# Batches 0 and 1 of a Fourier mixing layer and its MLP forward in plain float32, with a reordered start and a new tie rule in the planner

## Chip, cores and metric

The kernel runs on one core of one Trainium2 chip. The metric is the device time of one launch in microseconds (us), as the median of several runs. The core has a matrix engine (PE, whose weight loads are listed apart as PEld), a vector engine (DVE), a scalar engine (ACT), GpSimd (POOL), and the queue of SyncE (SP), which issues all transfers here.

## What is computed

The reference has two parts. The input x has 8 batches of 3136 positions and 256 features.

```python
X = np.fft.rfft(x, axis=1)
Yr = Xr @ w_r - Xi @ w_i + b_r
Yi = Xr @ w_i + Xi @ w_r + b_i
lam = 0.01
Yr = np.sign(Yr) * np.maximum(np.abs(Yr) - lam, 0.0)
Yi = np.sign(Yi) * np.maximum(np.abs(Yi) - lam, 0.0)
y = np.fft.irfft(Y, n=x.shape[1], axis=1)
...
h = x @ w_in
sm = e / (np.sum(e, axis=-1, keepdims=True) + 1e-09)
solu = h * sm
ln = (solu - mu) / np.sqrt(var + 1e-06) * g_ln
return (ln @ w_out).astype(np.float32)
```

In the second part x is the 25088 rows of the first part's result, w_in is 256 x 1024 in float64, w_out is 1024 x 256 in float64, and e = exp(h - max h).

## The kernel before

**Transform.** 3136 = 98 x 32, so each batch is transformed in two steps by matrices. Step 1 (`fwd1`, for batch 0 `fwd1_first`) multiplies 98 rows by a 98 x 98 matrix, in 8 chunks c of 1024 columns, and writes the result `s1` to DRAM. Step 2 works in 13 units u of up to 128 rows: `load_bin` brings a group of 4 row blocks (2 units) back as the tile `bin`; `fwd2` multiplies it by the matrices `fb` into the tiles Xh, Xl; `mix` multiplies these by the mixing weights (tile yt, then y, split into yh and yl); `inv1` multiplies by `gb` and writes `s2` to DRAM. `inv2` reads `s2` (tile zt), multiplies by the 98 x 98 matrix `ia` and writes a ring of rows (`ring_hi`, `ring_lo`) for the MLP.

**Precision.** Operands are split in a high and a low half in float16, and each product is three matrix multiplications: high by high, high by low, low by high. The split costs one ACT copy and one DVE operation (Xh/Xl, xh/xl, zout, av). The scale of a split comes from the largest value of the batch: `load_peak` reads the batch once for that (8 loads, 8 DVE reductions `peaks`) before `fwd1` reads it again. In batch 0, step 1 is already one float32 multiplication (`fa_s`); `split_bin` then splits what step 2 reads (the tile `av`).

**MLP.** 196 tiles k of 128 rows. `moe_head` computes h in two halves of 512 columns (PSUM tile `ph`, 6 multiplications each), its maximum (`nm`), and exp and product (tile u). `moe_turn` splits u (lh by ACT, ll by POOL) and turns both by transposing transfers (th, tl). `moe_tail` multiplies by w_out (PSUM tile `po`, 24 multiplications). w_in and w_out arrive as float64 words; `load_wide` turns 512 columns of them into float32 in seven DVE operations (five of one input, tiles lh, ll, junk, and two of two inputs) and one on POOL. There are eight such conversions: four for w_in (`moe_w_in`), four for w_out (`moe_w_out`); `finish_w_in` and `finish_w_out` then scale and split them.

**Order.** All operations are recorded by `Plan`, which decides their order by a simulation with fixed costs per operation. Each operation carries a key (`nc.key`); on each engine, among the operations that can start within a tolerance of the earliest one, the lowest key is taken. The engine whose operation starts first is served; at a tie the first in `ENGINES` wins. Some DVE operations and all of POOL's take turns at one modelled port (`op.port`), so DVE and POOL often tie. `nc.hold` makes a transfer wait for another operation (`raw[b, g]`, the load of group g of batch b). All instructions are issued by one helper, so every row has the same line (L339 before, L342 after) and groups are told apart by their tiles.

Of the kernel before, what the change touches and what calls it, by code (L numbers as in the profile page):

```python
# [39 lines left out]
def fft_constants():  # L40
# [49 lines left out]
    out = dict(fa=FA.astype(np.float32))  # L90
# [145 lines left out]
class Plan:  # L236
# [3 lines left out]
    ENGINES = ("tensor", "vector", "scalar", "gpsimd", "sync")  # L240
# [100 lines left out]
    def order(self):  # L341
# [107 lines left out]
def fft_mix_solu_kernel(ctx: ExitStack, tc, x, w_r, w_i, b_r, b_i, w_in, w_out, g_ln, fa, fa16, fb, fs, gb, gs, ia, out):  # L449
# [81 lines left out]
    def load_peak(b, c):  # L531

        n = S * D // P // NPK
        t = xp.tile([P, C1], F32, name="xt", bufs=3)[:, :n]
        if b == 1 and c < 3:

            nc.hold(raw[0, 4])
        nc.sync.dma_start(t, x[b].rearrange("s d -> (s d)").rearrange("(p c n) -> c p n", p=P, c=NPK)[c])
        note_peak(b, c, NPK, t)

    def set_scales(b):
# [18 lines left out]
        nc.vector.tensor_scalar(sc[:, 4:], sc[:, :1], S_SCALE, None, ALU.mult)  # L560
# [7 lines left out]
            x=sc[:, 0:1], s=sc[:, 4:], lam=(sc[:, 2:3], sc[:, 3:4]), mix=un[:, 2:3], bias=bias_y, y=un[:, 1:2]  # L568
# [35 lines left out]
    def fwd1_first(c):  # L604


        if c == 0:
            s1[0] = dram.tile([N1, N2, D], F32, name="s1f")
        n2 = C1 // D
        xt = mp.tile([P, C1], F32, name="u", bufs=4)[:N1]  # L610
        nc.sync.dma_start(xt, x[0].rearrange("(n1 n2) d -> n1 (n2 d)", n1=N1)[:, c * C1 : (c + 1) * C1])
        note_peak(0, c, N2 // n2, xt)
        av = fp.tile([P, C1], F32, name=("zout", "bin")[c % 2], bufs=2)[:N1]
        for h in range(C1 // HF):
            hs = slice(h * HF, (h + 1) * HF)
            pa = front_psum(0)
            nc.reserve(av[:, hs])
            nc.tensor.matmul(pa[:N1], fa_s, xt[:, hs], start=True, stop=True)
            nc.scalar.copy(av[:, hs], pa[:N1])
        nc.sync.dma_start(s1[0][:, c * n2 : (c + 1) * n2], av.rearrange("p (n d) -> p n d", d=D))  # L620
# [8 lines left out]
    def load_bin(b, g):  # L629

        if b:
# [4 lines left out]
        v = s1[0][: 4 * Q].rearrange("(q c) n d -> q (c n) d", c=4).rearrange("q r d -> r q d")  # L636
# [19 lines left out]
    def fwd2(b, u):  # L656
        n, K = unit_size(u)
        if b not in s2:
            s2[b] = dram.tile([N1, N2 * 2 * D], F16, name="s2")
        if n == 1:  # L660
            bt, gi, fw = fp.tile([K, 1, 2, D], F16, name="bin_s", bufs=1), 0, [fs_s]
            if b:
                nc.sync.dma_start(bt[:, 0], s1[b][4 * Q :].rearrange("c n t d -> (c n) t d"))
            else:
                t = fp.tile([K, 1, D], F32, name="bin_f", bufs=1)
                nc.sync.dma_start(t[:, 0], s1[b][4 * Q :].rearrange("c n d -> (c n) d"))
                split_bin(bt, t)
        else:
# [11 lines left out]
        with nc.together():  # L680
            for i in range(n):
                for dh in range(ND):
                    ds = slice(dh * P, (dh + 1) * P)
                    for k, (t, j) in enumerate(((0, 0), (0, 1), (1, 0))):
                        nc.tensor.matmul(pv[:, :, dh, i], bt[:, gi + i, t, ds], fw[i][:, j], start=k == 0, stop=k == 2)

        if b:
            nc.scalar.activation(xs[:, :, :n], pv[:, 1, :, :n], AF.Copy, scale=B_SCALE)
        for r in range(2) if n == 1 else [slice(0, 2)]:
            nc.scalar.activation(xh[:, r, :, :n], pv[:, r, :, :n], AF.Copy, scale=B_SCALE)  # L690
            nc.vector.scalar_tensor_tensor(xl[:, r, :, :n], pv[:, r, :, :n], B_SCALE, xh[:, r, :, :n], ALU.mult, ALU.subtract)
        if b:
            nc.vector.scalar_tensor_tensor(xs[:, :, :n], pv[:, 0, :, :n], B_SCALE, xs[:, :, :n], ALU.mult, ALU.add)
# [50 lines left out]
    def mix(b, u):  # L744
# [6 lines left out]
        y = fp.tile([P, 2, D], F32, name="y", bufs=1)  # L751
# [13 lines left out]
    def inv1(b, u0, u1):  # L765
# [173 lines left out]
    for c in range(NCH):  # L939
        fwd1_first(c)  # L940
# [64 lines left out]
    nc.sync.dma_start(fb_s[0], fb[:, :QG])  # L1005
# [169 lines left out]
```

## Time and profile before

| | |
|---|---|
| median of 3 runs | 1658.26 us (1657.31 to 1661.03) |
| profiled execution, its own time | 1657.71 us |
| its span in the trace | 1655.8 us |
| busy: PE, DVE, ACT, POOL | 1581.2, 1381.2, 1244.9, 1134.9 us |
| mean granted PE clock | 0.982 of full speed |

The span is the time from the first to the last instruction in the trace; 1.9 us of the execution lie around it. A busy share of an engine counts the time in which at least one of its instructions runs.

### The profile page before, as it was taken

The page shows a single profiled execution, that of the slowest core. Times are in us where ns is not written, and L with a number is a line of the kernel's source. Part 1 is how long each engine was busy: PE and PEld are TensorE (multiplying, and loading weights), DVE is VectorE, ACT ScalarE, POOL GpSimd, SP SyncE. Part 2 cuts the span into 40 slices and gives each one's busy share as a digit, 9 for nine tenths or more (in the row PEclk, how much of TensorE's full clock was granted, in tenths as well). Part 3 has the DMA queues.
Part 4 walks back from the last instruction along what each step waited for, and adds up shares of the span by engine and source line. Part 5 has one row for each costly group of instructions (what it writes and reads, how often), then busy time and mean ns, then how long its engine had stood idle before and what let it go on. Part 6 is the DMA issues. An engine that isn't in the chain of part 4 may idle for free.

```text
span 1655.8 us, 38277 instructions
## 1 busy us (share of the span) xinstructions
PE 1581.2 (95%) x13220; PEld 1116.7 (67%) x13220; DVE 1381.2 (83%) x3399; ACT 1244.9 (75%) x2511; POOL 1134.9 (69%) x1889
## 2 busy tenths in 40 slices
PE   5777999999999999999999999999999999999998
PEld 3344677668775677667776577766777677766765
DVE  4999888997899968998779987899689878877775
ACT  3567876886777767887678886888678876777886
POOL 1464586768776678766776577776777767777666
PEclk8897999999999999999999999999999999999999
DMA  6735995799659987799857997689956986658766
GB/s 219 263 125 162 209 219 140 186 253 187 141 122 208 245 161 138 161 236 203 179 122 158 247 209 162 112 208 251 184 134 156 188 185 144 126 115 160 149 130 116
DMA packets 531267, 290.24 MB, mean 175 GB/s; under 512 B 425758, under 2 KB 502016, under 8 KB 531072
## 3 DMA queue, kind: packets, MB, share of 16 engines
q1 hardware_dynamic: 531072, 287.80, 79.0%
q8 instruction: 103, 1.69, 0.5%
q14 instruction: 92, 0.75, 0.1%
HBM read 107.88 MB, written 77.07 MB: 112 GB/s over the span
## 4 chain that ended last, share of the span: by engine, by line
PE 73%; DVE 8%; DMA 8%; ACT 4%; POOL 3%; issue 3%; SPq 0%; DVEq 0%; ACTq 0%; POOLq 0%
PE po L339 25%; PE ph L339 24%; PE pf L339 22%; DMA tl<-ll 2%; DMA th<-lh 2%; PE pb L339 2%; DVE u L339 1%; POOL ll L339 1%; DMA xt<-in_x_dram 1%; DVE yt L339 1%; DMA u<-in_x_dram 1%; DVE nm L339 1%; DMA zt<-s 1%; ACT u L339 1%; ACT junk L339 1%
## 5 line engine op out<-in xcount | busy, mean ns | idle before, releaser
L339 POOL TENSOR_TENSOR ll<-u,lh 128x1024 f16<-128x1024 f32 x196 | 425.4, 2170 | 113.5 <-ACT lh L339 107.8
L339 PE MATMUL po<-wout,th 128*128 128x256 f16 x3136 | 374.1, 273 | 6.6 <-DMA th<-lh 4.5
L339 PEld LDWEIGHTS <-th 128*128 128x128 f16 x3136 | 303.8, 98 | 69.4 <-DMA th<-lh 7.6
L339 ACT ACTIVATE u<-ph,m,hsb 128x512 f32<-128x512 f32 x384 | 295.9, 777 | 61.4 <-DVE m L339 58.7
L339 DVE TENSOR_REDUCE nm<-ph 128x1 f32<-128x512 f32 x392 | 266.0, 686 | 85.2 <-PE ph L339 83.1
L339 DVE SCALAR_TENSOR_TENSOR u<-ph,ch,u 128x512 f32<-128x512 f32 x392 | 281.8, 746 | 22.4 <-ACT u L339 12.2
L339 PE MATMUL ph<-win_low,ring_lo 128*128 128x512 f16 x784 | 297.9, 380 | 1.1 <-DVE ring_lo L339 1.1
L339 PE MATMUL ph<-win_hi,ring_hi 128*128 128x512 f16 x784 | 298.3, 381 | 0.2 <-DVE u L339 0.2
L339 PE MATMUL ph<-win_lo,ring_hi 128*128 128x512 f16 x784 | 297.9, 380 | 0.0
L339 ACT CAST lh<-u 128x1024 f16<-128x1024 f32 x196 | 205.6, 1049 | 65.9 <-DVE u L339 59.0
L339 PEld LDWEIGHTS <-ring_hi 128*128 128x128 f16 x1568 | 149.3, 98 | 139.0 <-issue 6.9
L339 ACT ACTIVATE junk<-u,total 128x1024 bf16<-128x1024 f32 x196 | 226.5, 1155 | 14.8 <-POOL total L339 14.6
L339 PE MATMUL po<-wout,tl 128*128 128x256 f16 x1568 | 203.5, 273 | 6.7 <-DMA tl<-ll 6.5
L339 PEld LDWEIGHTS <-tl 128*128 128x128 f16 x1568 | 150.4, 98 | 45.5 <-DMA tl<-ll 11.2
L339 POOL TENSOR_TENSOR y<-yt,yc 128x512 f32<-128x512 f32 (+1 forms) x104 | 139.0, 1337 | 44.0 <-DVE yc L339 36.8
L339 POOL TENSOR_TENSOR yl<-y,yh 128x512 f16<-128x512 f32 (+1 forms) x104 | 127.8, 1229 | 49.5 <-ACT yh L339 47.2
L339 ACT ACTIVATE o<-po,r 128x256 f32<-128x256 f32 x196 | 93.0, 475 | 79.8 <-PE po L339 57.7
L339 PE MATMUL pf<-w_hi,Xl 128*128 128x256 f16 (+1 forms) x546 | 148.9, 273 | 1.1 <-DVE Xl L339 1.0
L339 PE MATMUL pf<-w_hi,Xh 128*128 128x256 f16 (+1 forms) x546 | 149.3, 273 | 0.6 <-DVE u L339 0.6
L339 PE MATMUL pf<-w_lo,Xh 128*128 128x256 f16 (+1 forms) x546 | 148.9, 273 | 0.0
L339 PEld LDWEIGHTS <-ring_lo 128*128 128x128 f16 x784 | 76.7, 98 | 94.4 <-DVE ring_lo L339 1.6
L339 PEld LDWEIGHTS <-Xh 128*128 128x128 f16 (+1 forms) x1196 | 114.5, 100 | 32.4 <-issue 11.8
(176 smaller groups left out, 2920.2 us busy)
## 6 DMA issues: line engine op xcount, KB each, us to landing
xt<-in_x_dram SPq DMA_DIRECT2D x112, 392.0 KB
zt<-s SPq DMA_DIRECT2D x64, 392.0 KB
s<-av SPq DMA_DIRECT2D x56, 392.0 KB
bin<-s SPq DMA_DIRECT2D x42, 512.0 KB
s<-zout SPq DMA_DIRECT2D x42, 512.0 KB
out_dram<-o SPq DMA_DIRECT2D x64, 98.0 KB
u<-in_x_dram SPq DMA_DIRECT2D x8, 392.0 KB
th<-lh SPq DMA_TRANSPOSE x196
```

The lines of the kernel that those rows point to most:

```text
L339: getattr(engine, name)(*args, **kw)
```

## The change

Batch 0 and batch 1 go forward in plain float32 in both steps (`PLAIN = 2`): one float32 multiplication takes the place of three in float16, against float32 copies of the matrices (`fbf`, `fsf`), which `load_bin` brings group by group, twice in all. The tile `bin` is used as it comes; the scale is applied when Xh and Xl are made. Batch 1's peaks are taken from the chunks that step 1 reads, so its 8 extra loads go. Batch 0 also goes back in float32 (`PLAIN_Z = 1`): its `zout` and `zt` are float32, with no low half, and `inv2` multiplies by `iaf`. The float32 `fa_s` is loaded first of all, and all 8 chunks of batch 0 have buffers of their own. The units of batch 0 get lower keys than the conversions of w_in. Batch 1's step 1 gets the keys from -40 on. The float16 matrices `fb` are loaded only after group 5 of batch 0. In the planner the tolerance goes from 1 to 50 ns and GpSimd becomes the first engine at a tie.

```diff
@@ class Plan
-    ENGINES = ("tensor", "vector", "scalar", "gpsimd", "sync")
+    ENGINES = ("gpsimd", "tensor", "vector", "scalar", "sync")
+    PATIENCE = 50.0
...
-                _, _, at, op = min((op.key, op.seq, at, op) for at, op in can if at <= first + 1.0)
+                _, _, at, op = min((op.key, op.seq, at, op) for at, op in can if at <= first + self.PATIENCE)
@@ step 1
+    nc.key = -300
     fa_s = load([N1, N1], fa, "fa_s")
+    nc.key = 0
...
-    def fwd1_first(c):
+    def fwd1_plain(b, c):
...
+        pool, name, bufs = (mp, "u", 4) if b == 0 and c % 2 == 0 else (xp, "xt", 4)
+        xt = pool.tile([P, C1], F32, name=name, bufs=bufs)[:N1]
+        if b and c < 4:
+            nc.hold(raw[0, 4])
+        nc.sync.dma_start(xt, x[b].rearrange("(n1 n2) d -> n1 (n2 d)", n1=N1)[:, c * C1 : (c + 1) * C1])
+        note_peak(b, c, N2 // n2, xt)
...
+            nc.tensor.matmul(pa[:N1], fa_s, xt[:, hs], start=True, stop=True)
+            nc.scalar.copy(to, pa[:N1])
@@ step 2
         raw[b, g] = nc.sync.dma_start(t, v[:, g * QG : (g + 1) * QG])
-        load_after(gb_s[g].rearrange("p u r t m -> p u (r t) m"), gb[:, g * QG // 2 : (g + 1) * QG // 2].rearrange("p u r t m -> p u (r t) m"), raw[b, g])
-        if g + 1 < Q // QG:
-            load_after(fb_s[g + 1], fb[:, (g + 1) * QG : (g + 2) * QG], raw[b, g])
-        return split_bin(xp.tile([P, QG, 2, D], F16, name="av"), t)
+        fbs[g] = fp.tile([P, QG, P], F32, name="fbf", bufs=2)
+        nc.sync.dma_start(fbs[g], fbf[:, g * QG : (g + 1) * QG])
+        if b == 0:
+            load_after(gb_s[g].rearrange("p u r t m -> p u (r t) m"), gb[:, g * QG // 2 : (g + 1) * QG // 2].rearrange("p u r t m -> p u (r t) m"), raw[b, g])
+        return t
...
-                    for k, (t, j) in enumerate(((0, 0), (0, 1), (1, 0))):
-                        nc.tensor.matmul(pv[:, :, dh, i], bt[:, gi + i, t, ds], fw[i][:, j], start=k == 0, stop=k == 2)
+                    if b >= PLAIN:
+                        for k, (t, j) in enumerate(((0, 0), (0, 1), (1, 0))):
+                            nc.tensor.matmul(pv[:, :, dh, i], bt[:, gi + i, t, ds], fw[i][:, j], start=k == 0, stop=k == 2)
+                    else:
+                        nc.tensor.matmul(pv[:, :, dh, i], bt[:, gi + i, ds], fw[i], start=True, stop=True)
@@ back
+            if b < PLAIN_Z:
+                zv = zo[:, gi : gi + m].rearrange("p (u i) e -> p u i e", i=n)[:, :, i]
+                nc.scalar.activation(zv, pv, AF.Copy, scale=Z_SCALE)
+                continue
...
+                    if b < PLAIN_Z:
+                        nc.tensor.matmul(pa[:, i * N1 : (i + 1) * N1], zt[:, i, es], iaf_s, start=True, stop=True)
+                        continue
@@ keys
-    nc.key = -128
-    moe_w_in(0)
-    nc.key = -120
-    moe_w_in(1, raw[0, 0])
+    nc.key = 0
+    load_fb()
+    nc.key = -110
+    moe_w_in(0, raw[0, 0])
+    nc.key = -90
+    moe_w_in(1, raw[0, 1])
...
-            front_a(1, 0, 0.3)
+            front_a(1, -40, 0.5)
```

**What it does to the order: the first transfers.** On the queue of SP, before, the float32 matrix `fa_s_131` stands seventeenth, behind twelve other small loads and four of batch 0's eight chunks (u tiles), and the fifth chunk comes behind it:

```order
L339 DMA fa16_s_122<-in_fa16_dram 98x196
L339 DMA ia_s_125<-in_ia_dram 98x294
L339 DMA fb0_127<-in_fb_dram 128x1024
L339 DMA gt_129<-in_moe_g_ln_dram 128x8x1
L339 DMA fa_s_131<-in_fa_dram 98x98
L339 DMA u_150<-in_x_dram 98x1024
L339 DMA s1f_154<-zout_145 98x1024
L339 DMA u_161<-in_x_dram 98x1024
```

After, these are the first rows of SP; the other four chunks follow at once, and the first store of `s1f` is the eighteenth row:

```order
L342 DMA fa_s_82<-in_fa_dram 98x98
L342 DMA u_101<-in_x_dram 98x1024
L342 DMA xt_103<-in_x_dram 98x1024
L342 DMA u_105<-in_x_dram 98x1024
L342 DMA xt_107<-in_x_dram 98x1024
```

So the matrix moved ahead of everything, and no chunk stands behind a store any more.

**The conversions and the units.** On DVE, before, the peak of w_in (`wpeak_562`) and the first conversion of w_out (raw words u_465) come ahead of the yt of unit 3 (yt_621):

```order
L339 SCALAR_TENSOR_TENSOR zout_547<-zout_547,pb_534 128x256
L339 TENSOR_REDUCE wpeak_562<-win_peak_308 128x1
L339 TENSOR_SCALAR lh_564<-u_465 128x512
L339 TENSOR_SCALAR ll_583<-u_465 128x512
L339 TENSOR_SCALAR lh_564<-lh_564 128x512
L339 TENSOR_SCALAR junk_590<-u_465 128x512
L339 TENSOR_SCALAR lh_564<-lh_564 128x512
L339 SCALAR_TENSOR_TENSOR th_595<-u_465,junk_590 128x512
L339 SCALAR_TENSOR_TENSOR ll_583<-lh_564,ll_583 128x512
L339 TENSOR_SCALAR lh_602<-u_519 128x512
L339 SCALAR_TENSOR_TENSOR yt_621<-pb_570,un_271,bias_y_284 128x512
```

After, the peak of w_in (`wpeak_1031`) comes behind the last unit's yt (yt_1006, 64 rows), and w_out's first conversion (u_821) has only begun there:

```order
L342 SCALAR_TENSOR_TENSOR yt_979<-pb_913,un_261,bias_y_279 128x512
L342 SCALAR_TENSOR_TENSOR ll_929<-lh_926,ll_929 128x512
L342 TENSOR_SCALAR lh_989<-u_821 128x512
L342 SCALAR_TENSOR_TENSOR yt_1006<-pb_962,un_261,bias_y_279 64x512
L342 TENSOR_REDUCE win_peak_430<-u_803 128x1
L342 TENSOR_REDUCE wpeak_1031<-win_peak_430 128x1
L342 TENSOR_SCALAR lh_989<-lh_989 128x512
L342 TENSOR_SCALAR ll_1038<-u_821 128x512
L342 TENSOR_SCALAR lh_989<-lh_989 128x512
```

All thirteen yt have moved ahead of it; three of the four conversions of w_in still lie between the units, the fourth at their end.

**The first MLP tile.** On DVE, before, the first `ring_lo` and the first maximum (nm_1517) come when the conversions are long done, among batch 1's step 1 (xl, av):

```order
L339 SCALAR_TENSOR_TENSOR xl_1459<-xt_1361,sc_1325,xh_1426 98x1024
L339 SCALAR_TENSOR_TENSOR ring_lo_1481<-ring_hi_1444,pf_1413 128x392
L339 SCALAR_TENSOR_TENSOR ring_lo_1481<-ring_hi_1444,pf_1430 128x392
L339 SCALAR_TENSOR_TENSOR ring_lo_1481<-ring_hi_1444,pf_1446 128x392
L339 SCALAR_TENSOR_TENSOR ring_lo_1481<-ring_hi_1444,pf_1464 128x392
L339 SCALAR_TENSOR_TENSOR av_1495<-pf_1483,av_1495 98x2x256
L339 SCALAR_TENSOR_TENSOR av_1495<-pf_1490,av_1495 98x2x256
L339 TENSOR_REDUCE nm_1517<-ph_1498 128x1
```

After, the first `ring_lo` stands right behind the last conversion of w_out (u_1123), and the reductions and sums of w_out (mx, yc) come between it and the first maximum (nm_1272):

```order
L342 TENSOR_SCALAR lh_1195<-lh_1195 128x512
L342 SCALAR_TENSOR_TENSOR tl_1221<-u_1123,junk_1210 128x512
L342 SCALAR_TENSOR_TENSOR ll_1200<-lh_1195,ll_1200 128x512
L342 SCALAR_TENSOR_TENSOR ring_lo_1240<-ring_hi_1223,pf_1205 128x392
L342 SCALAR_TENSOR_TENSOR ring_lo_1240<-ring_hi_1223,pf_1216 128x392
L342 TENSOR_REDUCE peaks_635<-xt_1186 98x1
L342 TENSOR_REDUCE mx_1166<-th_1183 128x1
L342 TENSOR_REDUCE top_1261<-peaks_635 98x1
L342 TENSOR_REDUCE mx_1166<-tl_1221 128x1
L342 TENSOR_TENSOR yc_1266<-th_1140,tl_1161 128x512
L342 TENSOR_REDUCE wpeak_1270<-mx_1166 128x1
L342 TENSOR_REDUCE nm_1272<-ph_1249 128x1
```

What follows w_out's conversion (its sums and its scaling) has moved behind the first maximum, and xl and av are gone.

## Rows read from the trace of the kernel before

**Rows 1.** Busy time of each engine in four stretches (start:end in us, length; columns named).

```profile
core 0: us, PE busy (x) PEld busy (x) DVE busy (x) ACT busy (x) POOL busy (x), PEclk, DMA share, GB/s
0.00:47.07 47.07, 24.83 (x70) 13.13 (x70) 24.29 (x54) 19.64 (x38) 7.53 (x12) 0.78 0.74 236
47.07:124.00 76.93, 60.92 (x441) 32.31 (x441) 73.14 (x126) 45.81 (x86) 44.48 (x30) 0.89 0.55 182
124.00:163.67 39.67, 30.22 (x170) 17.23 (x171) 36.55 (x88) 28.04 (x51) 16.94 (x22) 0.78 0.55 159
163.67:1655.80 1492.13, 1465.18 (x12540) 1054.01 (x12539) 1247.24 (x3136) 1151.38 (x2338) 1065.97 (x1827) 1.00 0.82 173
```

**Rows 2.** Timeline of PE, 8 to 48 us: start, length, instruction, [idle before <- releaser].

```profile
14.24 13.26 PE L339 MATMUL pb<-u,fa_s 98*98 98x512 f32 x24 [7.87 <-DMA fa_s<-in_fa_dram]
...
44.14 0.39 PE L339 MATMUL pb<-fb,av 128*128 128x128 f16 x2 [7.96 <-ACT av L339]
```

**Rows 3.** Timeline of DVE, 0 to 60 us: peaks of the first and fourth chunk.

```profile
4.47 1.22 DVE L339 TENSOR_REDUCE peaks<-u 98x1 f32<-98x1024 f32 x1 [3.49 <-DMA u<-in_x_dram]
...
9.10 1.22 DVE L339 TENSOR_REDUCE peaks<-u 98x1 f32<-98x1024 f32 x1 [0.47 <-DMA u<-in_x_dram]
```

**Rows 4.** Busy times of one stretch, columns as in rows 1.

```profile
18.00:38.80 20.80, 15.34 (x39) 6.34 (x38) 11.44 (x32) 13.74 (x29) 0.00 (x0) 0.91 0.80 274
```

**Rows 5.** Timeline of SP's queue, 34 to 44 us.

```profile
38.82 0.93 SPq L339 DMA_DIRECT2D bin<-s1f  x2
```

**Rows 6.** Timeline of PE, 79 to 98 us: step 2 of two units.

```profile
79.41 0.84 PE L339 MATMUL pb<-fb,av 128*128 128x128 f16 x12
...
95.28 0.83 PE L339 MATMUL pb<-fb,av 128*128 128x128 f16 x12
```

**Rows 7.** Timeline of weight loads (PEld) in float32, 128 columns each.

```profile
1.03 5.15 PEld L339 LDWEIGHTS po<-ones 128*128 128x128 f32 x24 [1.03 <-DVE mhalf L339]
...
35.79 0.29 PEld L339 LDWEIGHTS pb<-v,ones 1*128 1x128 f32 x2 [3.21 <-ACT w_hi L339]
```

**Rows 8.** DVE's groups, 47.07 to 124 us: xcount | busy us, mean ns | idle before.

```profile
L339 DVE SCALAR_TENSOR_TENSOR yt<-pb,un,bias_y 128x512 f32<-128x512 f32 x12 | 8.9, 742 | 1.7 <-PE pb L339 1.7
L339 DVE SCALAR_TENSOR_TENSOR av<-bin,sc,av 128x1024 f16<-128x1024 f32 x5 | 8.3, 1656 | 0.1
L339 DVE SCALAR_TENSOR_TENSOR Xl<-pb,Xh 128x512 f16<-128x512 f32 x12 | 8.2, 680 | 0.0
...
L339 DVE SCALAR_TENSOR_TENSOR zout<-zout,pb 128x256 f16<-128x256 f16 x20 | 7.5, 410 | 0.6 <-ACT zout L339 0.3
...
L339 DVE TENSOR_SCALAR junk<-u 128x512 uint32<-128x512 uint32 x6 | 5.7, 949 | 0.0
L339 DVE SCALAR_TENSOR_TENSOR ll<-lh,ll 128x512 uint32<-128x512 uint32 x6 | 5.0, 834 | 0.0
...
L339 DVE SCALAR_TENSOR_TENSOR win_lo<-u,win_sc,win_hi 128x1024 f16<-128x1024 f32 x2 | 2.6, 1341 | 0.0
L339 DVE TENSOR_SCALAR lh<-u 128x512 uint32<-128x512 uint32 x6 | 2.5, 412 | 0.0
```

**Rows 9.** Timeline of DVE, 122.5 to 126 us: the last unit's yt.

```profile
123.28 0.73 DVE L339 SCALAR_TENSOR_TENSOR yt<-pb,un,bias_y 64x512 f32<-64x512 f32 x1
```

**Rows 10.** DVE's groups, 124 to 163.67 us, columns as in rows 8.

```profile
L339 DVE SCALAR_TENSOR_TENSOR xl<-xt,sc,xh 98x1024 f16<-98x1024 f32 x5 | 8.0, 1620 | 0.6 <-ACT xh L339 0.6
L339 DVE TENSOR_REDUCE nm<-ph 128x1 f32<-128x512 f32 x9 | 6.2, 687 | 0.4 <-PE ph L339 0.2
L339 DVE SCALAR_TENSOR_TENSOR av<-pf,av 98x512 f16<-98x512 f32 x8 | 5.2, 679 | 0.0
L339 DVE SCALAR_TENSOR_TENSOR u<-ph,ch,u 128x512 f32<-128x512 f32 x6 | 4.3, 744 | 0.0
```

**Rows 11.** Timeline of PE, 163 to 198 us: the first po, and one group of `inv2` (24).

```profile
163.67 1.91 PE L339 MATMUL po<-wout,th 128*128 128x256 f16 x16 [0.97 <-DVE u L339]
...
196.21 1.24 PE L339 MATMUL pf<-ia_s,zt 98*128 98x98 f16 x24
```

More of the change, by code (lines that the diff above doesn't have):

```diff
@@ L88, in fft_constants @@
     GS = GS.reshape(2, 2 * N2, 2 * N2).transpose(1, 0, 2)
-    out = dict(fa=FA.astype(np.float32))
+    out = dict(fa=FA.astype(np.float32), fbf=FB.astype(np.float32), fsf=FS.astype(np.float32))
+    out["iaf"] = (IA * IA_SCALE).astype(np.float32)
     parts = dict(fa16=FA * A_SCALE, fb=FB, fs=FS, gb=GB * G_SCALE, gs=GS * G_SCALE, ia=IA * IA_SCALE)
@@ L448, in fft_mix_solu_kernel @@
 @with_exitstack
-def fft_mix_solu_kernel(ctx: ExitStack, tc, x, w_r, w_i, b_r, b_i, w_in, w_out, g_ln, fa, fa16, fb, fs, gb, gs, ia, out):
+def fft_mix_solu_kernel(ctx: ExitStack, tc, x, w_r, w_i, b_r, b_i, w_in, w_out, g_ln, fa, fbf, fsf, iaf, fa16, fb, fs, gb, gs, ia, out):
     nc = Plan(tc.nc)
@@ L533, in load_peak @@
         n = S * D // P // NPK
-        t = xp.tile([P, C1], F32, name="xt", bufs=3)[:, :n]
-        if b == 1 and c < 3:
-            nc.hold(raw[0, 4])
+        t = xp.tile([P, C1], F32, name="xt", bufs=4)[:, :n]
         nc.sync.dma_start(t, x[b].rearrange("s d -> (s d)").rearrange("(p c n) -> c p n", p=P, c=NPK)[c])
@@ L602, in fwd1 @@
         nc.sync.dma_start(s1[b][:, c * n2 : (c + 1) * n2], av)
-    def fwd1_first(c):
+    PLAIN, PLAIN_Z = 2, 1
+    def fwd1_plain(b, c):
         if c == 0:
-            s1[0] = dram.tile([N1, N2, D], F32, name="s1f")
+            s1[b] = dram.tile([N1, N2, D], F32, name="s1f")
         n2 = C1 // D
[L610 to L613, printed above, removed]
+        pool, name, bufs = (mp, "u", 4) if b == 0 and c % 2 == 0 else (xp, "xt", 4)
[4 more added lines that the diff above has]
+        note_peak(b, c, N2 // n2, xt)
+        whole = b or c < 6
+        if whole:
+            pool, name = (xp, "av") if b else ((fp, "zout"), (fp, "bin"), (xp, "av"))[c % 3]
+            av = pool.tile([P, C1], F32, name=name, bufs=2)[:N1]
+            parts = [(av, 0, n2)]
+        else:
+            parts = [(mp.tile([P, HF], F32, name=name, bufs=3)[:N1], i * n2 // 2, n2 // 2) for i, name in enumerate(("th", "tl"))]
         for h in range(C1 // HF):
             hs = slice(h * HF, (h + 1) * HF)
-            pa = front_psum(0)
-            nc.reserve(av[:, hs])
+            to = parts[0][0][:, hs] if whole else parts[h][0]
+            pa = front_psum(b)
+            nc.reserve(to)
             nc.tensor.matmul(pa[:N1], fa_s, xt[:, hs], start=True, stop=True)
-            nc.scalar.copy(av[:, hs], pa[:N1])
-        nc.sync.dma_start(s1[0][:, c * n2 : (c + 1) * n2], av.rearrange("p (n d) -> p n d", d=D))
+            nc.scalar.copy(to, pa[:N1])
+        for av, i, n in parts:
+            nc.sync.dma_start(s1[b][:, c * n2 + i : c * n2 + i + n], av.rearrange("p (n d) -> p n d", d=D))
     QG = 4
@@ L671, in fwd2 @@
                 bins[b, g] = load_bin(b, g)
-            bt, fw = bins[b, g], [fb_s[g][:, gi + i] for i in range(2)]
-        xh = fp.tile([P, 3, ND, 2, 2 * N2], F16, name="Xh16", bufs=2)
-        xl = fp.tile([P, 3, ND, 2, 2 * N2], F16, name="Xl", bufs=2)
+            bt, fw = bins[b, g], [(fb_s if b >= PLAIN else fbs)[g][:, gi + i] for i in range(2)]
+        xh = fp.tile([P, 3, ND, 2, 2 * N2], F16, name="Xh16", bufs=3)
+        xl = fp.tile([P, 3, ND, 2, 2 * N2], F16, name="Xl", bufs=3)
         xs = fp.tile([P, ND, 2, 2 * N2], F32, name="Xs", bufs=1) if b else None
@@ L750, in mix @@
         up, down = scales[b]["lam"]
[L751 removed]
+        y = fp.tile([P, 2, D], F32, name="y", bufs=2)
         if b == 0:
@@ L771, in inv1 @@
         g, gi = divmod(2 * u0, QG)
+        part, dtype = ((2, D), F16) if b >= PLAIN_Z else ((D,), F32)
         if n == 1:
-            zo, gi = fp.tile([K, 1, 2, D], F16, name="zs", bufs=1), 0
+            zo, gi = fp.tile([K, 1, *part], dtype, name="zs", bufs=1), 0
         else:
             if gi == 0:
-                zouts[b] = fp.tile([P, QG, 2, D], F16, name="zout")
+                zouts[b] = fp.tile([P, QG, *part], dtype, name="zout")
             zo = zouts[b]
```

70 lines of the change are left out of this document (41 added, 29 removed).

## The prediction

> **What bounds the kernel now.** First read the busy times in four stretches [rows 1]; the reader subtracts PE's busy time from each length. PE lacks 22.2 us up to 47.07, 16.0 us up to 124.00, 9.5 us up to 163.67, and 27.0 us in the 1492 us after that, 74.7 us in all. So the last stretch is PE's and gives back little. The first three are not: 163.67 us in which PE is idle for 47.7 us and runs, on the average, at a granted clock of 0.78 to 0.89.
>
> What ends the waits there differs. Up to 47.07 it is transfers: the first multiplication waited 7.87 us for `fa_s`, and the units began at 44.14, after the load of `bin` and its split on ACT [rows 2]. From 47.07 to 124.00 DVE is busy 73.14 of 76.93 us: the units and the conversions share it. From 124.00, the end of the last yt [rows 9], to the first po at 163.67 [rows 11] DVE is busy 36.55 of 39.67 us. I call these stages 1, 2 and 3.
>
> **Stage 1: the first transfers.** Batch 0's chunks landed 1.54 us apart, from 4.47 to 9.10 for the first four [rows 3]. With `fa_s` ahead I let the first land at 4.9 and the eighth at 4.9 + 7 x 1.54 = 15.7. PE follows (the last chunk's two multiplications end some 3 us later), so `fa_s` is waited for no more. What is left on the queue then, by the sizes of the tiles, is 0.52 MB of mixing weights, 0.26 of biases, 0.52 of two `fbf`, 0.25 of small matrices and 3.21 of stores of `s1f`, 4.76 MB. At the 274 GB/s of 18 to 38.8 us [rows 4] that takes 17.4 us: the last store lands at 33.1. Before, the load of `bin` was issued at 38.82 [rows 5] and step 2 began 5.3 us later; 1.1 of that was ACT's split, which is gone. So the units start at 33.1 + 4.2 = 37.3. Bounds: at 330 GB/s 34, with the queue stalling as before 41.
>
> **Stage 2: the units.** DVE loses `av` (8.3 us) and nearly all `zout` (7.5) [rows 8], gains nothing per unit, and keeps only w_in's four conversions. It then owes: Xl and yt 17.1 us, a little more for the last unit, four conversions, win_peak 2, and four peaks of 1.22 [rows 3]. A conversion is five one-input operations, 0.412 us each when nothing blocks them (the lh row) and 0.949 when POOL is in the way (the junk row), and two two-input ones of 0.68 to 0.83 [rows 8], so 3.4 to 6.4 us; beside busy units I take 4.8. Sum 44 us. PE owes more: from 79.41 to 95.28, when nothing held it long, four units took 15.87 us [rows 6], 3.97 each.
>
> In float32 a unit's step 2 is 4 multiplications instead of 12. Two float32 loads of 128 columns with almost no columns to stream lie about 0.108 us apart (0.29 us for both, 0.18 the second) at the granted clock of 1.0 there; with 128 columns to stream, 24 passes at the start took 5.15 us, one each 0.21 [rows 7], PE then as slow as at 1.2 GHz by its later rows. A multiplication makes two passes, so I price it 0.215 at 2.4 GHz: 0.86 for four, against 12 x 128 columns at 2.4 GHz = 0.64. A unit costs 3.97 + 0.22 = 4.19 us. Twelve and a half make 52.4, and PE, idle before, runs the first few us at 1.2 GHz: 2.5 more. The last mix ends at 92.2, its yt at 92.9 instead of 124.0: 31.1 us gained.
>
> The Trainium skill (TensorE: Matmul & The Clock Gate, Weight-path perf modes — Fast Weight Load (FWL) and DoubleRow) says that float32 weights get no fast load, and its section LDWEIGHTS that a load's time goes by the columns of the weights; this speaks against `inv2` in float32, whose 98 columns stream faster than 128 load. The pair of loads 0.108 us apart [rows 7] agrees. By streamed columns alone, `inv2` would come out about 2 us cheaper than I price it below.
>
> **Stage 3: w_out and the first tiles.** The order puts w_out behind the units, so part of the gain goes back: DVE must finish it before the first po. Against the 36.55 us busy of before, these go: five xl 8.0, eight av 5.2, two of nine nm 1.4, three of six u 2.2 [rows 10], and five zout 2.0 [rows 8]. These come: w_out's four conversions but for one operation, 14.0 at 3.6 (POOL has less to do here; bounds 3.4 and 4.8), two win_lo 2.7, five peaks 5.8, five reductions of w_in and w_out at the price of nm 3.4. That is 43.7. The 3.1 us of waits stay, and the last scaled part of w_out still needs a cast on ACT and a subtraction on POOL before PE can use it, 1.8. So 48.5 us instead of 39.7, and the first po starts at 141.4 instead of 163.67: 22.3 us earlier. Meanwhile PE does batch 1's step 1 (16 float32 multiplications of 512 columns, four times 512 columns at 2.4 GHz = 0.85 each, 13.7 us), which costs nothing under this cover; uncovered it would cost 16 x (0.85 - 0.64) = 3.4.
>
> **After the first po.** By the order, both kernels have done 54 ph multiplications when it starts. Of batch 1's step 1 the new one has nothing left, the old one 18 passes of 512 columns, 3.8 us. Step 2 of batch 1 costs 50 x 0.215 - 150 x 0.053 = 2.7 more. Of `inv2` of batch 0, 40 multiplications are left, 8.6 us, where 132 were left at 0.045 (24 in 1.24 us, less the 0.2 in which the last drains [rows 11]), 5.9: 2.7 more. Sum +1.6. The float32 matrices are 1.6 MB more to load for each of two batches, and 3.2 MB of peaks fall away: nothing, at a DMA share of 0.82 [rows 1].
>
> **The planner's two numbers** move rows in all of the 196 tiles. What they can give back is at most the 27.0 us that PE lacks after 163.67. What they can cost has no such limit. Counting by the order the PE work between a tile's last ph and its first po, I find it about as long as before (20.7 before and 20.4 now on the mean of tiles 29 to 56), so I take 0, and 6 us either way for the range.
>
> **Sum.** -22.3 + 1.6 = -20.7 us. From the profiled execution's 1657.71 us (span 1655.8) this gives 1637; the median of the runs shown, 1658.26, lies 0.5 above that execution, which I neglect. By 0.2%, about 3.3 us, a measurement of this kernel can tell a change from none.
>
> **Rivals.**
> *The units are paced by their chain, not by PE.* From 47.07 to 79.41 five and a half units took 32 us, 5.9 each, while conversions lay among them; the new order still has four among thirteen. If half the units go at 5.9, stage 2 grows by 12.5 x 0.86 = 11 us: 1648. One mechanism for it is the port. The junk row's 0.949 against 0.412 shows DVE standing behind POOL; POOL's 44.48 us in stage 2 [rows 1] and 13.6 us of unblocked conversions, one after the other, would make 58.1 us against my 54.9, and waits of the chain come on top. The Trainium skill (SBUF — State Buffer, SBUF: two separate sides) calls that port an exclusive lock that is held for a whole instruction; the 0.949 us agrees, though most of the units' DVE work reads PSUM and did not slow (Xl 0.680). Against this rival: at 79 to 95 us PE did run through.
> *More comes back.* Stage 3 has fewer waits (3 us), transfers run at 330 GB/s (3), and the new order halves the 27 us after the first po (about 6 for a quarter): 1625.
> *The new order costs more in the tiles than the start gains.* Each of 196 tiles has to wait for its turned operand (th, tl). If ll on POOL or u on DVE comes 0.11 us later per tile without cover, 196 x 0.11 = 21 us are gone, and from 0.13 us on the kernel is slower: 1662. For it: two numbers that touch every tile. Against it: the same PE order around each po, and ACT, DVE and POOL all have 16% or more to spare there [rows 1].
> *Nothing is won.* Stage 3 takes 70 us, because w_out's loads stand on SP behind the six `fb` loads (1.5 MB, held until group 5 has come) and behind stores of `s2` that wait for units; DVE, in order, stands at the conversion, and ring_lo, nm and with them PE behind it: 1658. For it: the last w_in words are queued there too. Against: by my count w_out's words are needed 10 us after the units end, and a transfer needs some 4.
>
> **How the numbers follow.** The sum as written 0.54 (1630 to 1644); chain 0.19 (to 1654); more 0.14; costlier tiles 0.08; nothing won 0.05. 1621 to 1654 takes in the bounds of stages 1 to 3 and all cases but about 2 in 10. Faster by over 0.2% has 0.54 + 0.19 + 0.14 = 0.87, within it 0.05, slower 0.08.
>
> **What would show it.** First fa_s multiplication before 6 us and without waiting for fa_s; first step 2 near 37; the last yt near 93, with PE busy over 90% from 45 to 90; DVE busy over 90% from 93 to 140; first po near 141; then a PE idle sum near 27. Batch 0's step 2 passes 0.107 apart. I am wrong if step 2 in float32 runs at 0.107 only when loads are hidden and they are not (0.43 per multiplication, +10 us a batch), if DVE idles in stage 3, or if PE's idle time after the first po moves by over 10 us.

## The result and the profile after

The changed kernel takes 1635.74 us in the median of 4 runs (1632.69 to 1638.63), the kernel before 1658.30; the ratio is 0.9865, with a 95% interval of 0.984 to 0.9889. The forecast was 1637. Two of its executions took 1632.7 and 1633.0 us and two 1638.5 and 1638.6; the profiled one is of the longer pair (1638.51, span 1636.7), 2.8 us above the median.

The same four stages as in [rows 1], cut at the changed kernel's own marks (busy time of each engine, then PE's granted clock, DMA share, GB/s; a clock of 1.00 is 2.4 GHz, 0.50 is 1.2):

```profile
core 0: us, PE busy (x) PEld busy (x) DVE busy (x) ACT busy (x) POOL busy (x), PEclk, DMA share, GB/s
0.00:36.54 36.54, 20.62 (x68) 11.49 (x68) 16.55 (x37) 17.12 (x35) 3.46 (x10) 0.84 0.82 243
36.54:93.40 56.86, 56.86 (x380) 34.33 (x382) 40.09 (x64) 34.98 (x67) 32.92 (x27) 0.95 0.75 245
93.40:144.10 50.70, 41.11 (x177) 22.66 (x173) 42.33 (x116) 32.49 (x68) 22.53 (x21) 0.83 0.76 229
144.10:1636.70 1492.60, 1467.65 (x12420) 1059.28 (x12420) 1218.36 (x3130) 1149.99 (x2327) 1070.40 (x1833) 1.00 0.82 171
```

PE idles 15.9 us, nothing, 9.6 and 25.0 us in them, where it idled 22.2, 16.0, 9.5 and 27.0. In the second stage PE is busy without a gap. The gain is all ahead of the first po: the last stretch is as long as before, 1492.60 against 1492.13 us.

The marks themselves, from PE's timeline (start, length, instruction, [idle before <- releaser]); they answer to [rows 2, 6, 11]:

```profile
5.51 1.93 PE L342 MATMUL pb<-u,fa_s 98*98 98x512 f32 x4
...
36.54 5.49 PE L342 MATMUL pb<-fbf,bin 128*128 128x128 f32 x24 [13.50 <-DMA bin<-s1f]
...
113.44 7.12 PE L342 MATMUL pf<-iaf_s,zt 98*128 98x98 f32 x32 [8.36 <-DMA zt<-s2f]
...
135.76 1.92 PE L342 MATMUL pf<-iaf_s,zt 98*128 98x98 f32 x16
...
144.14 1.92 PE L342 MATMUL po<-wout,th 128*128 128x256 f16 x16 [1.28 <-DVE ch L342]
```

and the last yt, from DVE's timeline, which answers to [rows 9]:

```profile
92.72 0.74 DVE L342 SCALAR_TENSOR_TENSOR yt<-pb,un,bias_y 64x512 f32<-64x512 f32 x1 [0.68 <-PE pb L342]
```

| mark | before | forecast | after |
|---|---|---|---|
| first multiplication by fa_s | 14.24 | before 6 | 5.51 |
| units start | 44.14 | 37.3 | 36.54 |
| end of the last yt | 124.0 | 92.9 | 93.46 |
| first po | 163.67 | 141.4 | 144.14 |
| from the first po to the end | 1492.1 | +1.6 | 1492.6 |

The reader sees two things in the rows. In the units PE now runs without a gap. And between 93 and 144 us there is a wait that the forecast did not have: PE stands 8.36 us for the first zt, and after it runs `inv2` at the lower clock, 32 passes in 7.12 us where 16 take 1.92 later.

### The profile page after: what moved, and what is told of

It reads as the page before. It is cut to its first block, busy times and chain, and to the rows that moved or that the text cites. A ratio compares the mean times of both kernels' runs of the same rounds, so it can differ in the third digit from the quotient of the medians.

```text
span 1636.7 us, 37871 instructions
## 1 busy us (share of the span) xinstructions
PE 1586.2 (97%) x13040; PEld 1127.8 (69%) x13040; DVE 1317.3 (80%) x3343; ACT 1234.6 (75%) x2496; POOL 1129.3 (69%) x1889
## 4 chain that ended last, share of the span: by engine, by line
PE 78%; DMA 8%; DVE 5%; ACT 3%; POOL 2%; issue 2%; SPq 0%; DVEq 0%; ACTq 0%; POOLq 0%
PE po L342 26%; PE ph L342 24%; PE pf L342 23%; PE pb L342 4%; DMA th<-lh 4%; DMA tl<-ll 3%; DVE u L342 1%; POOL ll L342 1%; ACT junk L342 1%; DVE xl L342 1%; ACT lh L342 1%; DVE nm L342 1%; ACT u L342 0%; DMA zt<-s 0%; DVE av L342 0%
## 5 line engine op out<-in xcount | busy, mean ns | idle before, releaser
L342 PE MATMUL po<-wout,th 128*128 128x256 f16 x3136 | 375.3, 273 | 10.6 <-DMA th<-lh 9.2
L342 PEld LDWEIGHTS <-th 128*128 128x128 f16 x3136 | 303.8, 98 | 74.5 <-DMA th<-lh 15.8
L342 POOL TENSOR_TENSOR y<-yt,yc 128x512 f32<-128x512 f32 (+1 forms) x104 | 133.0, 1279 | 61.0 <-ACT yt L342 32.7
```

Source lines behind the costliest of these rows:

```text
L342: getattr(engine, name)(*args, **kw)
```

## How the experiments are compared

Total times are medians, with their ratios to runs of the kernel before on the same chip (whose median lay between 1658.3 and 1660.9 us). For the start one more number is needed, because a new order may put more or less of PE's work ahead of the first po. I call it PE's arrears: the time at which ACT begins the output of tile 0, less the PE work that the order puts ahead of that tile's last po, counted in columns at 2.4 GHz (float32 four times, and at least 0.215 us for each multiplication; those by gb half, since four of 256 columns take the time of two). It is worked out from the order and one trace. Before it is 75.2 us, after 43.6. By the same count the whole program holds 1494.9 us of PE work before and 1509.7 after, the price of float32: -31.6 + 14.8 - 2.4 (what the tiles after it add) = -19.2, the difference of the two spans, rounded. The last term is what the spans leave over, so that this sum closes by its making.

Units, yt, po and arrears in the table are those of the one profiled execution of each run. It can lie off the median: that of peaks_three_times took 1655.27 us, 9.0 more than its median. Where the text takes the difference of two medians, the ratios can give up to 4 us less, because the runs of the kernel before differ too.

| run | median us | ratio (95%) | units start | start of last yt | first po | arrears |
|---|---|---|---|---|---|---|
| before | 1658.3 | | 44.1 | 123.3 | 163.7 | 75.2 |
| changed | 1635.7 | 0.9865 (0.9840 to 0.9889) | 36.5 | 92.7 | 144.1 | 43.6 |
| old_tie_rule | 1646.3 | 0.9913 (0.9891 to 0.9935) | 37.5 | 98.1 | 150.1 | 46.1 |
| new_tie_rule_alone | 1645.9 | 0.9910 (0.9892 to 0.9929) | 44.5 | 103.9 | 158.1 | 62.0 |
| gpsimd_first_alone | 1647.7 | 0.9922 (0.9898 to 0.9946) | 44.2 | 103.0 | 156.8 | 61.8 |
| tolerance_alone | 1656.4 | 0.9987 (0.9964 to 1.0009) | 44.3 | 118.8 | 161.8 | 73.2 |
| units_first_alone | 1657.2 | 0.9980 (0.9965 to 0.9995) | 43.9 | 112.0 | 158.9 | 74.7 |
| w_in_ahead | 1632.7 | 0.9831 (0.9807 to 0.9856) | 35.3 | 93.0 | 145.3 | 42.1 |
| batch1_in_float16 | 1654.3 | 0.9959 (0.9943 to 0.9974) | 36.2 | 91.5 | 177.0 | 65.5 |
| batch1_float16_old_keys | 1651.6 | 0.9936 (0.9908 to 0.9963) | 36.8 | 91.2 | 153.4 | 51.3 |
| batch0_back_in_float16 | 1638.0 | 0.9858 (0.9836 to 0.9881) | 35.8 | 91.3 | 161.4 | 45.8 |
| fa_s_later | 1641.4 | 0.9885 (0.9861 to 0.9909) | 45.0 | 101.2 | 152.7 | 52.4 |
| peaks_three_times | 1646.2 | 0.9921 (0.9893 to 0.9949) | 39.6 | 104.4 | 161.6 | 61.2 |
| batch1_step1_later | 1634.4 | 0.9835 (0.9812 to 0.9858) | 36.3 | 92.3 | 156.6 | 44.6 |

## Experiments: the planner's two numbers

The prediction gave these two numbers 0 within 6 us. Here the changed kernel is run with the old ones, the kernel before with the new ones, and each new number alone on the kernel before.

```diff
 # old_tie_rule, on the changed kernel
-    ENGINES = ("gpsimd", "tensor", "vector", "scalar", "sync")
-    PATIENCE = 50.0
+    ENGINES = ("tensor", "vector", "scalar", "gpsimd", "sync")
+    PATIENCE = 1.0
```

**old_tie_rule.** Expected: 

> The changed kernel with the planner's two old numbers (TensorE first at a tie, tolerance 1 ns); all else as changed. My theory, by which these two numbers are worth about nothing: 1636 us, between 1630 and 1642, and the last yt of batch 0 near 93 us as with the change. Rival, by which the tie rule makes a large part of the 22 us: 1646 us or more, and PE's idle time after the first po larger by 10 us or more.

Measured: 1646.31 us. My theory fell. The rival's time came out, but not its place: after the first po PE idles 27.1 us, where it idles 24.9 in the changed kernel, so not 10 more (columns as in [rows 1]):

```profile
150.07:1645.10 1495.03, 1467.96 (x12394) 1056.40 (x12392) 1229.90 (x3110) 1143.79 (x2317) 1062.59 (x1819) 1.00 0.80 169
```

The arrears are 2.5 us more. Of the 8.4 us between the two profiled spans the other 5.9 come behind tile 0; what makes them is not shown.

```diff
 # new_tie_rule_alone, on the kernel before (gpsimd_first_alone: the first line only; tolerance_alone: the second only)
-    ENGINES = ("tensor", "vector", "scalar", "gpsimd", "sync")
+    ENGINES = ("gpsimd", "tensor", "vector", "scalar", "sync")
-... if at <= first + 1.0)
+... if at <= first + 50.0)
```

**new_tie_rule_alone.** Expected: 

> The kernel before with nothing but the planner's two new numbers. My theory: 1658 us, within 6 either way, since DVE still has all its conversions and splits to do before the first tiles can run freely. Rival (the tie rule makes the gain): 1646 us or less.

Measured: 1645.91 us. My theory fell. The arrears at tile 0 are 62.0 instead of 75.2, 13.2 us less; what the tiles add after it is the same (86.1 and 85.8). So the gain of these numbers on the kernel before is in the start, not in the tiles.

**gpsimd_first_alone.** Expected: 

> The kernel before with GpSimd as the first engine at a tie, the tolerance left at 1 ns. By the order its start is that of the kernel with both numbers: five conversions ahead of the last yt instead of eight, and 108 ph multiplications before the first po instead of 54. My theory now: the tie order alone makes the gain, because GpSimd's part of the units no longer stands behind a DVE conversion at the port. 1647 us (1644 to 1650). Rival, by which the tolerance makes it: 1656 us or more.

**tolerance_alone.** Expected: 

> The kernel before with the tolerance at 50 ns, TensorE first at a tie. By the order its start is that of the kernel before (eight conversions ahead of the last yt, 54 ph before the first po). My theory now: 1659 us, within 4 either way. Rival (the tolerance makes the gain): 1648 us or less.

Measured: 1647.68 us for GpSimd first, with arrears of 61.8, and 1656.41 for the tolerance, whose interval holds no change. So the gain is the order at a tie. What it does to GpSimd can be read from POOL's groups, 47 to 124 us, first in the kernel before, then with the new numbers (xcount | busy us, mean ns | idle before it):

```profile
L339 POOL TENSOR_TENSOR yl<-y,yh 128x512 f16<-128x512 f32 x11 | 18.3, 1661 | 24.9 <-ACT yh L339 24.9
L339 POOL TENSOR_TENSOR y<-yt,yc 128x512 f32<-128x512 f32 x12 | 17.6, 1468 | 0.9 <-ACT yt L339 0.4
```

```profile
L340 POOL TENSOR_TENSOR y<-yt,yc 128x512 f32<-128x512 f32 (+1 forms) x13 | 16.9, 1303 | 6.7 <-ACT yt L340 4.7 <-PE pb L340 1.7
L340 POOL TENSOR_TENSOR yl<-y,yh 128x512 f16<-128x512 f32 (+1 forms) x13 | 16.2, 1247 | 12.0 <-ACT yh L340 12.0
```

GpSimd's two operations of a unit take 2.55 us instead of 3.13. It stands 12.0 us instead of 24.9 for yh, and 6.7 instead of 0.9 ahead of y: 18.7 us in all instead of 25.8. In the order five conversions of eight stand ahead of the last yt on DVE where all eight did, and twice as many ph multiplications (108 for 54) stand ahead of the first po, because the heads of the first tiles now go before batch 1's splits (the first xl starts at 160.9 us; before, at 131.2). How the 13 us divide between the units and the heads was not tried.

## Experiments: the units ahead of the weights

```diff
 # units_first_alone, on the kernel before (w_in_ahead: the reverse, on the changed kernel)
-    nc.key = -128
+    nc.key = -110
     moe_w_in(0, ...)
-    nc.key = -120
+    nc.key = -90
     moe_w_in(1, ...)
```

**units_first_alone.** Expected: 

> The kernel before with nothing but the new keys of w_in's conversions (-110 and -90), so that the units of batch 0 go ahead of them; float16 splits remain. My theory: DVE owes the same work before the first po (134 us busy up to there, against 99 in the changed kernel), so it gains only what DVE idled: the last yt of batch 0 comes 10 to 20 us earlier, the first po at most 4 us earlier, 1655 us. Rival (the order of units and conversions is what gains): first po 12 us or more earlier, 1646 us or less.

Measured: 1657.22 us; the last yt comes 11.3 us earlier, the first po 4.8 (I had allowed 4), and the arrears are 0.5 less. Its stages 2 and 3:

```profile
47.00:112.00 65.00, 55.23 (x418) 28.98 (x416) 63.41 (x113) 38.25 (x74) 36.09 (x27) 0.96 0.66 220
112.00:158.90 46.90, 28.24 (x174) 16.70 (x174) 43.48 (x98) 27.63 (x51) 20.95 (x24) 0.67 0.36 100
```

DVE is busy 98% and 93% of them: what the units win, the conversions give back, as expected.

**w_in_ahead.** Expected: 

> The changed kernel with w_in's conversions at their old keys (-128 and -120), ahead of the units by key. By the order, with the new tie rule only one conversion moves ahead in the first eight units. My theory: the tie rule, not these keys, keeps the conversions out of the units' way: 1637 us, within 3 either way. Rival (the keys do it): 1643 us or more.

Measured: 1632.68 us, 1.3 below the range that I had expected, and the rival, 1643 or more, falls. With GpSimd first at a tie these keys do nothing that costs.

## Experiments: what float32 is worth

```diff
 # batch1_in_float16 (batch0_back_in_float16: 2, 0)
-    PLAIN, PLAIN_Z = 2, 1
+    PLAIN, PLAIN_Z = 1, 1
 # batch1_float16_old_keys: the line above, and
-            front_a(1, -40, 0.5)
+            front_a(1, 0, 0.3)
```

In the two with PLAIN = 1 the first four loads for batch 1's peaks are held until group 4 of batch 0 has come (before the change the first three were).

**batch1_in_float16.** Expected: 

> The changed kernel with batch 1 forward in float16 as before (PLAIN = 1), batch 0 still plain. My theory: DVE gets back 8 xl of 1.62 us and some 16 av of 0.68 us, 24 us, about two thirds of it before the first po and without cover there; PE saves about 5 us of float32 prices. The first po comes 8 to 14 us later than 144, the whole 1644 us (1639 to 1650). Rival (batch 1's step 1 stands beside other waits anyway, the transfers of stage 3 set the first po): 1634 us or less.

Measured: 1654.28 us, 18.5 more than the changed kernel (some 16 by the ratios) and above the range that I had expected. The first po comes 33 us later, not 8 to 14. DVE's groups from 93 to 177 us, the first po:

```profile
L342 DVE SCALAR_TENSOR_TENSOR av<-pf,av 98x512 f16<-98x512 f32 x16 | 10.7, 685 | 3.7 <-ACT av L342 3.7
L342 DVE SCALAR_TENSOR_TENSOR xl<-xt,sc,xh 98x1024 f16<-98x1024 f32 x8 | 10.2, 1275 | 0.0
```

All 16 av and all 8 xl stand ahead of the first po, 20.9 us, and the arrears grow by 21.9.

**batch1_float16_old_keys.** Expected: 

> The changed kernel with batch 1 forward in float16 (PLAIN = 1) and with the old keys of its step 1 (0 in steps of 0.3), so that its 24 us of xl and av on DVE need not all go ahead of the first tiles. My theory: the 18 us that batch 1 in float16 cost came half from these 24 us of DVE, half from the key -40 that puts all of them ahead of the first po: 1646 us (1642 to 1650), first po well before 177. Rival (where they stand does not matter, DVE owes them in the start): 1652 us or more.

Measured: 1651.59 us in the median of 5 runs (1644.57 to 1655.40), between the two theories and 0.4 us from the rival's bound. The arrears are 51.3, 14.2 less than with the key -40, and its profiled execution, with a span of 1642.8, is the shortest of the five. The place of the splits decides the start by this one execution. In the whole it does not show: batch1_step1_later, below, has these same old keys in float32, and against it batch 1 in float16 costs 17.2 us, with the key -40 it costs 18.5. Either way it is over 10 us.

**batch0_back_in_float16.** Expected: 

> The changed kernel with batch 0 going back in float16 (PLAIN_Z = 0): 26 zout on DVE come back, 10.7 us, most of them beside the units; inv2 is three float16 multiplications again, 64 x (0.215 - 0.135) = 5.1 us less of PE. My theory after the run with the repeated peaks (added DVE work beside the units cost nearly its own length): 7 us later at the first po by the same PE work, 5 less to do, 1638 us (1634 to 1643). Rival, as the prediction had it (PE covers DVE beside the units): 1632 us or less.

Measured: 1637.99 us, the time that I expected, but not for my reason. The arrears grow by 2.2 us, not 7 (the first po itself moves to 161.4, because 108 ph multiplications now stand ahead of it instead of 54). DVE's groups beside the units, 35.8 to 92.1 us:

```profile
L342 DVE SCALAR_TENSOR_TENSOR Xl<-pb,sc,Xh 128x512 f16<-128x512 f32 x12 | 9.0, 747 | 13.5 <-ACT Xh L342 13.2
...
L342 DVE SCALAR_TENSOR_TENSOR zout<-zout,pb 128x256 f16<-128x256 f16 x18 | 6.9, 412 | 3.7 <-ACT zout L342 3.7
```

The 18 zout lie in time in which DVE would wait for ACT; the last yt does not move (91.3). PE covers them, as the prediction had it. Whether batch 0 goes back in float32 or in float16 makes no difference that the two intervals can tell.

## Experiments: the first loads, DVE in stage 3, batch 1's step 1

```diff
 # fa_s_later
-    nc.key = -300
+    nc.key = 0
     fa_s = load([N1, N1], fa, "fa_s")
 # peaks_three_times
-        nc.vector.tensor_reduce(peaks[b][:, c : c + 1], t, AX.X, ALU.max, ...)
+        op = nc.vector.tensor_reduce(peaks[b][:, c : c + 1], t, AX.X, ALU.max, ...)
+        if b == 1:
+            op.calls += op.calls * 2
 # batch1_step1_later
-            front_a(1, -40, 0.5)
+            front_a(1, 0, 0.3)
```

**fa_s_later.** Expected: 

> The changed kernel with fa_s loaded at the place that its key 0 gives it, eighteenth on SP's queue behind the eight chunks and all small loads; DVE's and PE's order are unchanged. My theory: the first fa_s multiplication starts near 18.5 us, PE's 13.8 us of step 1 end at 32.3 instead of 19.4, the last store of s1f is issued 4 to 5 us later, the units start at 41 instead of 36.5, all that follows is shifted by it: 1640 us. Rival (stage 1 is bound by its bytes alone, so the place of one small load does not matter): units at 36.5, 1636 us.

Measured: 1641.37 us. From PE's timeline and SP's:

```profile
20.50 3.70 PE L342 MATMUL pb<-u,fa_s 98*98 98x512 f32 x4 [3.08 <-DMA fa_s<-in_fa_dram]
23.99 3.24 PE L342 MATMUL pb<-xt,fa_s 98*98 98x512 f32 x4
27.07 1.88 PE L342 MATMUL pb<-u,fa_s 98*98 98x512 f32 x4
```

```profile
41.08 0.94 SPq L342 DMA_DIRECT2D bin<-s1f  x2
```

The bytes are the same, and the units start 8.4 us later, not 4.5: step 1 also runs its first two chunks at the lower clock, after a wait of PE (3.70 and 3.24 us where the third takes 1.88; the granted clock is 0.50 from 18.0 to 24.0 us and 1.00 from 27.0), and the stores of s1f are now issued as PE ends its chunks, 1.72 us apart. So PE's step 1 becomes the bound of stage 1 as soon as fa_s is late; the rival falls. Of the 8.4 us the median shows 5.6 (3 by the ratios, whose intervals overlap).

**peaks_three_times.** Expected: 

> The changed kernel with each of batch 1's eight peak reductions done three times on DVE (the planner is not told, so no order changes; the output is the same). Four of them lie between 93 and 144 us, so DVE gets 8 x 1.13 = 9 us more there; the other four lie beside the units, under PE. My theory (DVE sets the first po in stage 3): first po at 153, 1645 us. Rival (the way of the last s2f store, the first zt load and inv2 sets it, and DVE's 8.4 us of waits there absorb the rest): first po at 147 or earlier, 1638 us or less.

Measured: 1646.24 us, near the 1645 of my theory and far from the rival's 1638. The profiled execution is the longest of the four, though: 1655.27 us, where the others took 1645.4 to 1646.8. Its stages 2 and 3, and then those of the changed kernel, cut at the same marks:

```profile
39.60:105.20 65.60, 59.40 (x382) 34.62 (x384) 49.82 (x72) 35.38 (x68) 32.45 (x27) 0.91 0.66 214
105.20:161.60 56.40, 42.09 (x176) 22.41 (x173) 52.12 (x122) 32.15 (x68) 18.63 (x21) 0.82 0.70 205
```

```profile
36.54:93.50 56.96, 56.96 (x382) 34.42 (x384) 40.19 (x64) 35.08 (x68) 33.02 (x27) 0.95 0.75 245
93.50:144.10 50.60, 41.01 (x175) 22.57 (x171) 42.23 (x115) 32.40 (x68) 22.43 (x21) 0.83 0.76 228
```

In this execution stage 3 grows by 5.8 us for some 9 us of DVE work: DVE sets most of it, and some 3 us go into its waits. But stage 2 grows by 8.6 us too, which neither theory had. DVE still idles 15.8 us of it. PE now waits, 4.7 us for Xl and 1.4 for Xh, and is busy 2.4 us longer at a mean clock of 0.91 instead of 0.95; three reductions in a row, 3.4 us, stand ahead of a unit's operation on DVE. The 18 zout of the run above are 6.9 us as well and cost nothing there, since they lie one by one where DVE waits. The start of this execution, 39.6, is 3.1 us later than in the changed kernel, before any added work. Together the first po comes 17.4 us later, where the median grew by 10.5. The other executions can hardly have lost all of this, so that the row of reductions costs stage 2 in them too is not shown.

**batch1_step1_later.** Expected: 

> The changed kernel with the old keys of batch 1's step 1 (0 in steps of 0.3 instead of -40 in steps of 0.5). By the order 96 ph multiplications stand before the first po instead of 54, and all of batch 1's step 1 still does. Theory A (the start is one account of DVE's work and PE's, and its order inside it moves little): 1636 us, within 3 either way. Theory B (batch 1's peaks and transfers stand in the way of w_out and of the first zt): 1630 us or less. Theory C (step 1 filled PE's wait for zt and now takes PE time of its own): 1642 us or more.

Measured: 1634.39 us, theory A. The first po is 12.5 us later and the arrears are 1.0 more: by the first po alone one would have called this a loss.

Two of these versions, w_in_ahead and batch1_step1_later, came out 3.1 and 1.4 us below the changed kernel in the median. Their intervals overlap with its own, so that they are not shown to beat it.

## Why the prediction was right, step by step

**Stage 1** (37.3; measured 36.54). Right, with both halves: the chunks came first, and fa_s was not waited for. The reason was told too simply. I counted bytes; fa_s_later shows that PE's step 1 lies close behind them.

**Stage 2** (92.9; 93.46). From the start of the units to the end of the last yt it is 56.9 us, against 55.6 as forecast. PE is busy all the time, DVE 40.1 us of 56.9 where I had counted 44. The float32 price holds. 16 passes of step 2 take 1.95 us and 16 of `inv2` 1.92, less the 0.2 in which the last drains: 0.109 and 0.108 each, 0.218 and 0.215 for a multiplication.

```profile
47.13 1.95 PE L342 MATMUL pb<-fbf,bin 128*128 128x128 f32 x16
```

Both load 128 columns of weights, but step 2 streams 128 columns and `inv2` 98, so the streamed columns do not set the price of `inv2`. The Trainium skill (TensorE: Matmul & The Clock Gate, Weight-path perf modes — Fast Weight Load (FWL) and DoubleRow) says that float32 weights gain nothing from the fast load; the equal prices agree. The lower clock after the wait, estimated at 2.5 us, is the first row here:

```profile
36.50:42.00 5.50, 5.46 (x25) 5.37 (x26) 1.50 (x2) 1.37 (x2) 0.00 (x0) 0.50 0.76 256
...
105.00:113.40 8.40, 0.08 (x1) 0.00 (x0) 6.24 (x15) 2.77 (x6) 5.72 (x2) 0.61 0.90 306
113.40:125.00 11.60, 11.56 (x42) 8.80 (x43) 9.65 (x19) 4.88 (x11) 2.54 (x2) 0.54 0.63 207
```

5.5 us at 1.2 GHz are 2.75 lost.

**Stage 3** (48.5 us; measured 50.7 from the end of the last yt to the first po). DVE's work was sized right, 42.3 us for 43.7, its waits not: 8.4 us where I had 4.9. So DVE was busy 83% and not over 90%, which the prediction had named as a sign of being wrong: this step is right in its mechanism and 3.5 us short in its waits. What it waited for, from its list of waits from 93.4 to 144.1 us (in total, times, longest):

```profile
DVE mx L342 <- ACT th L342: 2.2, 1, 2.2
DVE v L342 <- PE pf L342: 1.5, 1, 1.5
DVE win_un L342 <- PE pf L342: 1.3, 1, 1.3
DVE win_lo L342 <- ACT win_hi L342: 1.0, 1, 1.0
```

Beside DVE runs a second chain that the forecast did not price: the last store of s2f, the first zt (PE waits 8.36 us), and `inv2` and the first heads at the lower clock (the third row above, 11.6 us at 0.54). peaks_three_times shows DVE as the stronger of the two, by its one profiled execution.

**After the first po** (+1.6; +0.5). Right in size: PE is busy 2.5 us longer there, and idles 2.0 less, which the forecast had held equal.

**The planner's two numbers** (0 within 6). This is the step that failed, in its place: "What they can give back is at most the 27.0 us that PE lacks after 163.67." On the kernel before they act ahead of that time: they are worth some 13 to 15 us, 13.2 by the arrears, and the tiles add the same. On top of the rest of the change they are worth 10.6 us in the medians (8 by the ratios), of which the arrears show 2.5. That the sum held is no merit of this step. It held because its marks (which conversions stand ahead of which yt, 54 ph ahead of the first po) were read from the order of the changed kernel, which has the new numbers in it; I put to the units' keys and to float32 what partly belongs to the tie. The parts overlap: the tie rule alone gives a ratio of 0.9910, all the rest alone 0.9913, which would make 29 us together, and both give 22.6.

No run takes back batch 0's forward float32 alone, so its share of the gain stays open.

**The rivals.** None came true. The one that had the units paced by their chain through the port is not shown by old_tie_rule either. With the old tie rule the units take 61.3 us instead of 56.9, and GpSimd's yl 1434 ns instead of 1237, but PE idles no more than 0.2 us in them. What PE does there in addition is 8 passes of batch 1's step 1, 3.4 us at 0.43 each (the stretch with columns as in [rows 1], then PE's group in it: xcount | busy us, mean ns | idle before):

```profile
37.50:98.80 61.30, 61.14 (x385) 35.64 (x386) 46.83 (x76) 37.48 (x73) 36.79 (x27) 0.95 0.78 255
...
L342 PE MATMUL pf<-xt,fa_s 98*98 98x512 f32 x8 | 4.2, 602 | 0.0
```

More did not come back, the tiles did not become dearer, and something was won.

## What to carry to other kernels

A rule of a planner acts wherever engines tie, and that may be mostly the start, so run such a number by itself on the old kernel before its effect is put to anything else. Gains of parts that relieve the same engine do not add. At a start that DVE bounds, one float32 multiplication for three in float16 pays although it costs PE more (here 14.8 us by the count), as long as DVE's split is what goes; and the time of the first output is no measure of a start when the order around it changes. A profile is of one execution: set its time beside the median before a stage of it is read as the cause.

## What the runs showed of the hardware

One GpSimd operation here took four times its usual length beside a whole row of DVE operations. From POOL's timeline of the changed kernel:

```profile
104.45 5.05 POOL L342 TENSOR_TENSOR th<-th,ll 128x512 f32<-128x512 f32 x1 [5.42 <-DVE th L342]
109.46 1.26 POOL L342 TENSOR_TENSOR tl<-tl,ll 128x512 f32<-128x512 f32 x1
```

and from DVE's:

```profile
105.41 0.42 DVE L342 TENSOR_SCALAR lh<-lh 128x512 uint32<-128x512 uint32 x1
...
107.95 0.42 DVE L342 TENSOR_SCALAR lh<-u 128x512 uint32<-128x512 uint32 x1
110.54 0.69 DVE L342 TENSOR_REDUCE mx<-th 128x1 f32<-128x512 f32 x1 [2.16 <-ACT th L342]
```

An operation of the same shape takes 1.26 us right after it. Counted back from its end, 109.50, those 1.26 us begin at 108.24, where DVE's row of seven operations on SBUF without a gap comes to its end (108.37); that the one ended the other's wait is read from these times alone, and what GpSimd did from 104.45 to 105.41, beside a reduction on DVE (`peaks`), they do not say. DVE then pays for it with 2.16 us of waiting for the th that GpSimd held up. The Trainium skill (SBUF — State Buffer, SBUF: two separate sides) speaks of a lock for a whole instruction; here the operation was held up by some 3.8 us, the length of several.
